# Moving all transposes of a chunk-selected attention and gated MLP kernel from the matmul engine to the DMA crossbar

## The chip, the cores and the metric

The kernel runs on one core of one Trainium2 chip. The metric is the device time of one execution, in microseconds (us), as the median of several executions. Some executions fall into a slower state of the chip; here one counts as slow when it took over 1.5% longer than the fastest of the same kernel.

The names of the engines are those of the profile. PE is the matmul engine, PEld its weight load, DVE the vector engine, ACT the scalar engine, POOL the general engine (GpSimd), SP the sync engine, which here only starts DMAs.

## The reference, cut to what matters

For each of 4 batches there are 8 heads with 768 tokens and 64 columns. An attention picks, for each query, 6 of 24 key chunks by an upper bound on the score. Its output goes through a gated MLP that mixes over tokens.

```python
k_min, k_max = min and max of k over each chunk of 32 keys
ub   = sum_d maximum(q*k_min, q*k_max)            # bound for each query and chunk
sel  = the 6 chunks with the largest ub among the causal ones
mask = sel & (key <= query)
attn = softmax(where(mask, q.k / 8, -1e9)); x = attn @ v      # [768, 512] a batch
h = relu(x @ w_in); u, v = h[:, :512], h[:, 512:]
v_n = (v - mean(v)) / sqrt(var(v) + 1e-6)
v_s = w_spatial @ v_n + b_spatial[:, None]        # mixes tokens
out = (u * v_s) @ w_out
```

## The kernel before

Work goes in pairs of heads, 4 pairs a batch, 16 in all. `prep(i)` makes the operands of pair `i` and its selection, `attend(i)` does scores, exponentials and the product with v. The MLP of a batch is cut into pieces that are put between the attention steps of the next batch; the MLP of the last batch runs alone at the end.

Every transpose is done by PE: it multiplies by an identity, the result lands in PSUM, and DVE or ACT copies it to SBUF.

```python
def load(i):                                  # 6 loads a pair, 96 KB each, issued by POOL
    for hi in range(2):
        nc.gpsimd.dma_start(out=kp[:, :, hi, :], in_=view(k))
        nc.gpsimd.dma_start(out=qs[:, :, hi, c0:c0 + D], in_=view(q))
        nc.gpsimd.dma_start(out=vt[:, :, hi, 0:D], in_=view(v))

def prep(i):
    for t in range(NQT):                      # keys: 6 blocks of 128x128
        nc.tensor.transpose(tr[:, t * P:(t + 1) * P], kp[:, t, :, :], identity)
    ... # DVE: chunk max and min from tr; ACT: keys from tr into kh
    ... # queries: 6 blocks on PE; DVE: relu(q), relu(-q)
    ... # PE: bound ub; DVE: top 6, selection written into free columns of qs
    for hi in range(2):                       # queries + selection: 12 blocks
        for t in range(NQT):
            nc.tensor.transpose(tr[:, t * P:(t + 1) * P], qs[:, t, hi, :], identity)
        nc.vector.tensor_copy(ah, tr)

def attend(i):
    ...
        mm(sc[:, col:col + n], lhsT=kh[hi][:, t * P:(t + 1) * P], rhs=a[hi][:, q0:q0 + n],
           start=True, stop=not dg)
        if dg:                                # causal triangle, added by a matmul
            mm(sc[:, col:col + P], lhsT=identity, rhs=tri, start=False, stop=True)
    nc.scalar.activation(out=e[...], in_=sc[...], func=Act.Exp, scale=scale)
    ... # PE: e @ v; DVE: divide; PE + DVE: 6 blocks of x transposed into xT

# MLP of a batch; the gate comes out already transposed (columns on partitions)
def s_piece(db):
    for (t0, t1) in HALVES:                   # 512 and 256 tokens
        for si in range(NQT):
            mm(vs[:, 0:t1 - t0], lhsT=st["vn"][:, si, db * P:(db + 1) * P], rhs=wsT[:, si, t0:t1], ...)
        mm(vs[:, 0:t1 - t0], lhsT=brow_l, rhs=brow[:, t0:t1], start=False, stop=True)   # bias
        nc.vector.tensor_tensor(st["gT"][:, db, t0:t1], in0=vs[...], in1=st["uT"][...], op=Alu.mult)

load(0); load(1); load_weights(); prep(0)
for i in range(NPAIR):
    load(i + 2); prep(i + 1); attend(i)
    if i == 1: prep_weights()                 # 36 blocks of w_spatial, on PE
    ...                                       # MLP pieces of the batch before
```

The softmax here doesn't subtract the row's maximum and nothing guards it: scores larger than these inputs give would overflow.

## Time and profile before

The median of the three runs is 289.61 us (288.96 to 293.75).

| before | value | view |
|---|---|---|
| span, busy PE / DVE / ACT / POOL | 287.5; 222.4 / 170.7 / 154.3 / 98.1 us | page, part 1 |
| granted clock over the run | 0.976 | clock of the core |
| first exponential; the first one of the pair's second head | 27.5; 44.0 us | timeline of ACT |
| first MLP step of the four batches | 86.9, 147.3, 207.5, 257.1 us | timeline of ACT |
| data moved by DMA | 18.86 MB in 80,590 packets | page, part 2 |

These are the parts of the page of before on which the argument rests. In the line below the span each engine has its busy time, its share of the span and its number of instructions. In the rows below it, each digit is one of 40 slices of the span and gives the busy share in tenths (0 is under a tenth). The DMA row gives the same for the mean of the core's 16 DMA engines, and the last lines give packets, MB and the time of the packets as a share of 16 engines' span.

```profile
span 287.5 us, 5812 instructions
PE 222.4 (77%) x2340; PEld 144.9 (50%) x2340; DVE 170.7 (59%) x498; ACT 154.3 (54%) x217; POOL 98.1 (34%) x150
PE   0037028787879798989798989978888989799994
PEclk9999758999999999999999999999999999999999
DMA  0999997879996667558984848079220000140005
q0 software_dynamic: 77104, 12.20, 57.3%
q1 hardware_dynamic: 3460, 6.30, 6.0%
kp<-in_k_dram POOLq DMA_DIRECT2D x32, 96.0 KB, 3.3
```

From the seventh slice on, PE is busy 70 to 90% in nearly every slice, and at nearly the full clock. The loads of q, k, v and the weights are in queue q0. Their packets occupied 57.3% of the span's DMA time, and the DMA row falls under 9 in most slices from the thirteenth on: DMA had room. A load of 96 KB landed 3.3 us after its issue.

These are lines of the timeline of before in its first 45 us, with start, duration, engine, operation and, in brackets, the idle time ahead and what ended it.

```profile
27.51 1.02 ACT L217 ACTIVATE e<-sc 128x1024 f16<-128x1024 f32 x1 [8.57 <-PE sc L216]
35.13 0.83 POOL L140 DMA_DIRECT2D kp<-in_k_dram  x1 [5.43 <-DMA ws_raw<-in_moe_w_spatial_dram]
40.09 0.20 PE L177 MATMUL acc<-km,rq 128*128 128x48 f16 x1 [11.01 <-POOL km L161]
44.02 1.02 ACT L217 ACTIVATE e<-sc 128x1024 f16<-128x1024 f32 x1 [11.96 <-PE sc L216]
```

The start has a hole: after the first head's exponentials ACT idles until 44.0 us. POOL's later load issues wait until the weight loads have landed, and the small `km` product on POOL stands behind them; PE waits 11.0 us for `km` before it goes on to the second head's scores.

### The profile page before, as it was taken

The page shows a single profiled execution, that of the slowest core. Times are in us where ns is not written, and L with a number is a line of the kernel's source. Part 1 is how long each engine was busy: PE and PEld are TensorE (multiplying, and loading weights), DVE is VectorE, ACT ScalarE, POOL GpSimd, SP SyncE. Part 2 cuts the span into 40 slices and gives each one's busy share as a digit, 9 for nine tenths or more (in the row PEclk, how much of TensorE's full clock was granted, in tenths as well). Part 3 has the DMA queues.
Part 4 walks back from the last instruction along what each step waited for, and adds up shares of the span by engine and source line. Part 5 has one row for each costly group of instructions (what it writes and reads, how often), then busy time and mean ns, then how long its engine had stood idle before and what let it go on. Part 6 is the DMA issues. An engine that isn't in the chain of part 4 may idle for free.

```text
span 287.5 us, 5812 instructions
## 1 busy us (share of the span) xinstructions
PE 222.4 (77%) x2340; PEld 144.9 (50%) x2340; DVE 170.7 (59%) x498; ACT 154.3 (54%) x217; POOL 98.1 (34%) x150
## 2 busy tenths in 40 slices
PE   0037028787879798989798989978888989799994
PEld 0025016666655565655465656655546565544551
DVE  8337005888788875565579865474688654238330
ACT  1021405775785868146878674086878660656213
POOL 9995264546562434124243424051200000000000
PEclk9999758999999999999999999999999999999999
DMA  0999997879996667558984848079220000140005
GB/s 1 65 120 199 194 127 52 56 49 71 70 65 41 46 41 47 37 64 65 204 55 31 55 31 57 0 81 222 16 15 3 0 2 0 39 182 2 0 0 219
DMA packets 80590, 18.86 MB, mean 66 GB/s; under 512 B 75698, under 2 KB 76978, under 8 KB 80564
## 3 DMA queue, kind: packets, MB, share of 16 engines
q0 software_dynamic: 77104, 12.20, 57.3%
q1 hardware_dynamic: 3460, 6.30, 6.0%
q8 instruction: 18, 0.29, 0.4%
q14 instruction: 8, 0.07, 0.1%
HBM read 24.39 MB, written 6.29 MB: 107 GB/s over the span
## 4 chain that ended last, share of the span: by engine, by line
PE 50%; ACT 23%; DMA 8%; POOL 7%; DVE 7%; issue 3%; ACTq 0%; DVEq 0%; POOLq 0%
ACT e L217 13%; PE acc L322 11%; PE sc L213 7%; PE acc L310 7%; DMA w_out_sb<-in_moe_w_out_dram 6%; PE acc L224 5%; PE acc L333 5%; PE acc L285 5%; DVE stats L289 2%; PE tr L234 2%; POOL kp L140 2%; PE sc L216 2%; DMA out_dram<-o 2%; ACT uT L312 2%; PE acc L324 2%
## 5 line engine op out<-in xcount | busy, mean ns | idle before, releaser
L217 ACT ACTIVATE e<-sc 128x1024 f16<-128x1024 f32 (+1 forms) x96 | 84.0, 916 | 44.0 <-PE sc L216 42.9
L140 POOL DMA_DIRECT2D kp<-in_k_dram x32 | 26.7, 839 | 54.1 <-PE tr L152 48.0
L224 PEld LDWEIGHTS <-e 128*128 128x128 f16 x672 | 27.0, 98 | 31.3 <-ACT e L217 17.8
L216 PE MATMUL sc<-tri,identity 128*128 128x128 f16 x192 | 39.5, 222 | 0.0
L336 ACT COPY o<-acc 128x512 f32<-128x512 f32 x24 | 14.0, 585 | 46.9 <-PE acc L333 44.8
L322 PE MATMUL acc<-wsT,vn 128*128 128x512 f16 (+1 forms) x192 | 37.2, 325 | 0.4 <-ACT uT L312 0.2
L325 DVE TENSOR_TENSOR gT<-acc,uT 128x512 f16<-128x512 f32 (+1 forms) x32 | 17.8, 557 | 20.0 <-PE acc L324 18.8
L155 DVE TENSOR_REDUCE kmm<-tr 128x24 f16<-128x768 f16 x16 | 15.3, 953 | 20.4 <-PE tr L152 20.3
L322 PEld LDWEIGHTS <-vn 128*128 128x128 f16 x192 | 18.2, 98 | 12.2 <-issue 1.1
L310 PE MATMUL acc<-xT,w_in_sb 128*128 128x512 f16 (+1 forms) x128 | 23.4, 325 | 0.9 <-ACT uT L312 0.7
L333 PE MATMUL acc<-w_out_sb,gT 128*128 128x512 f16 x96 | 23.1, 378 | 0.4 <-ACT o L336 0.3
L216 PEld LDWEIGHTS <-identity 128*128 128x128 f16 x192 | 19.0, 99 | 7.4 <-issue 5.7
L285 PE MATMUL acc<-w_in_sb,xT 128*128 128x512 f16 x96 | 22.2, 379 | 0.0
L177 PE MATMUL acc<-km,rq 128*128 128x48 f16 x160 | 9.6, 188 | 15.9 <-POOL km L161 14.5
L152 PE MATMUL tr<-identity,kp 128*128 128x128 f16 x96 | 10.0, 229 | 14.7 <-DMA kp<-in_k_dram 14.6
L312 ACT ACTIVATE uT<-acc 128x512 f16<-128x512 f32 (+1 forms) x32 | 14.3, 488 | 12.4 <-PE acc L310 12.3
L289 DVE BATCH_NORM_STATS2 stats<-vraw 128x6 f32<-128x512 f32 x24 | 16.6, 694 | 6.1 <-ACT vraw L287 6.1
L227 DVE RECIPROCAL rec<-acc 128x6 f32<-128x6 f32 x32 | 6.1, 190 | 22.9 <-PE acc L224 22.9
L287 ACT ACTIVATE vraw<-acc 128x512 f32<-128x512 f32 x24 | 14.3, 597 | 9.6 <-PE acc L285 9.6
L180 DVE TENSOR_TENSOR acc<-acc,cmask 128x40 f32<-128x40 f32 x16 | 3.3, 208 | 25.6 <-PE acc L177 22.7
L161 POOL TENSOR_TENSOR km<-kmm,hmask 128x48 f16<-128x48 f16 x32 | 8.3, 276 | 26.3 <-DVE kmm L155 22.6
L310 PEld LDWEIGHTS <-w_in_sb 128*128 128x128 f16 x128 | 12.1, 97 | 9.7 <-issue 1.3
(236 smaller groups left out, 452.0 us busy)
## 6 DMA issues: line engine op xcount, KB each, us to landing
out_dram<-o SPq DMA_DIRECT2D x24, 256.0 KB, 2.0
kp<-in_k_dram POOLq DMA_DIRECT2D x32, 96.0 KB, 3.3
qs_90<-in_q_dram POOLq DMA_DIRECT2D x12, 96.0 KB, 3.3
vt_96<-in_v_dram POOLq DMA_DIRECT2D x12, 96.0 KB, 3.0
ws_raw<-in_moe_w_spatial_dram POOLq DMA_DIRECT2D x1, 1152.0 KB, 15.1
w_in_sb<-in_moe_w_in_dram POOLq DMA_DIRECT2D x1, 1024.0 KB, 10.3
qs_98<-in_q_dram POOLq DMA_DIRECT2D x10, 96.0 KB, 3.2
vt_104<-in_v_dram POOLq DMA_DIRECT2D x10, 96.0 KB, 3.1
```

What stands on the lines that cost most here:

```text
L140: nc.gpsimd.dma_start(out=kp[:, :, hi, :], in_=view(k))
L213: mm(sc[:, col:col + n], lhsT=kh[hi][:, t * P:(t + 1) * P], rhs=a[hi][:, q0:q0 + n], start=True, stop=not dg)
L216: mm(sc[:, col:col + P], lhsT=identity, rhs=tri, start=False, stop=True)
L217: nc.scalar.activation(out=e[:, BASES[g]:BASES[g] + WIDTHS[g]], in_=sc[:, 0:WIDTHS[g]], func=Act.Exp, scale=scale)
L224: mm(avv[:, qi, :], lhsT=e[:, c:c + P], rhs=vt[:, t, hi, 0:D + 1], start=(t == 0), stop=(t == qi))
L285: mm(hv, lhsT=x[:, ko, bi * P:(bi + 1) * P], rhs=w_in_sb[:, ko, DH:DFF], start=(ko == 0), stop=(ko == NDO - 1))
L289: nc.vector.bn_stats(stats, st["vraw"][:, bi, :])
L310: mm(hu[:, 0:t1 - t0], lhsT=w_in_sb[:, ko, db * P:(db + 1) * P], rhs=x[:, ko, t0:t1], start=(ko == 0), stop=(ko == NDO - 1))
L312: nc.scalar.activation(st["uT"][:, db, t0:t1], hu[:, 0:t1 - t0], func=Act.Relu)
L322: mm(vs[:, 0:t1 - t0], lhsT=st["vn"][:, si, db * P:(db + 1) * P], rhs=wsT[:, si, t0:t1], start=(si == 0), stop=False)
L325: nc.vector.tensor_tensor(st["gT"][:, db, t0:t1], in0=vs[:, 0:t1 - t0], in1=st["uT"][:, db, t0:t1], op=Alu.mult)
L333: mm(o_ps, lhsT=st["gT"][:, db, ti * P:(ti + 1) * P], rhs=w_out_sb[:, db, :], start=(db == 0), stop=(db == KO - 1))
```

## The change

The intent was to take from PE everything that is not a product of data, and to remove the hole at the start:

- All transposes go to the DMA crossbar, started by SP: keys, queries, queries with selection, x, w_spatial, and (new) the gate. Keys then come to SBUF, so that DVE and no longer ACT copies them to their places.
- POOL zeroes the triangle in the exponentials, in place of 192 matmuls that add a large negative number to the scores.
- The MLP has tokens on partitions throughout, so its bias is a scalar of a partition. The gate `g` must then be transposed to `gT` before the output matmul, 4 blocks for each 128 tokens.
- There is one load for each tensor and pair (192 KB, 3 a pair); loads and preparation run one pair further ahead; in the program, the weight loads come after the first attention.

The core of the diff, with cuts:

```diff
+    def transpose(out_, in_):
+        nc.sync.dma_start_transpose(out=out_, in_=in_)
...
-        for t in range(NQT):
-            nc.tensor.transpose(tr[:, t * P:(t + 1) * P], kp[:, t, :, :], identity)
+        transpose(kT..., kp...)                       # 6 blocks
+        transpose(qT..., qp...)                       # 6 blocks
-        nc.scalar.copy(kh[0][D:2 * D, :], tr[0:D, :])
-        nc.scalar.copy(kh[1][0:D, :], tr[D:2 * D, :])
+                nc.vector.tensor_copy(dst[:, sp], kT[s0:s1, hi])      # 4 a pair
+            nc.vector.tensor_copy(qs[:, hi, :, d0:d1], qp[:, 2 * j + hi])
...
-        for hi in range(2):                           # selection on PE, copied by DVE
+        a = sb.tile([P, 2, S], F16, tag="a", name="a", bufs=3)
+        transpose(a..., qs...)                        # 12 blocks
...
-                    if dg:
-                        mm(sc[:, col:col + P], lhsT=identity, rhs=tri, start=False, stop=True)
+            for c0, n, w in ((0, 4, 512), (1920, 2, 384)):
+                nc.gpsimd.affine_select(out=blk, in_=blk, compare_op=Alu.is_ge, fill=0.0, ...)
...
+        def s_piece(ti):                              # tokens on partitions
+                nc.vector.scalar_tensor_tensor(g, in0=vs, scalar=bT[:, ti:ti + 1], in1=st["u"][:, ti, :],
+                                               op0=Alu.add, op1=Alu.mult)
+                gT = ml.tile([P, KO, P], F16, tag="gT", name="gT", bufs=3)
+                transpose(gT, g)                      # 4 blocks
...
+        pieces += [s_piece(0), s_piece(1)]
+        for ti in range(2, NQT):
+            pieces += [o_piece(ti - 2), s_piece(ti)]
+        pieces += [o_piece(NQT - 2), o_piece(NQT - 1)]
...
-    load(0); load(1); load_weights(); prep(0)
+    load(0)                                           # ahead of the constants
+    load(1); prep(0); load(2); prep(1)
-    # attend(i) follows load(i + 2) and prep(i + 1)
+    # attend(i) follows load(i + 3) and prep(i + 2); weights are loaded after attend(0)
```

## The prediction

> **What bounds the kernel now.** The matmul engine, in steady state. The table by stretches shows PE busy 16.6 to 18.6 us of every 20 us from 80 to 240 us (DVE 10.5 to 16.4, ACT 10.0 to 16.4). The chain of waits gives PE 50%, ACT 23%. Two other losses. The start: up to 40 us PE is busy 8.2 us; the timeline shows the first exponential at 27.5 us, then a hole to 44.0 us, because POOL's queue waits for the weight loads (w_in, ws_raw, w_out) before later loads and before the small km products. The end: from 252 us the last batch's MLP runs alone, 35 us. A batch in steady state takes about 60 us (first MLP matmul at 148.3, the next at 208.4 us).
>
> **What is removed.** PE: all transposes (k, q, selection, x, w_spatial) and the triangle and bias matmuls. Columns: 13,960 to 8,680 for a pair of heads, 58,400 to 55,300 for an MLP. At the trace's pace (512 columns every 0.21 us) about 200 us of issue fall to about 158. ACT: 32 key copies, 25.5 us; 154 to about 130. DVE: copies of transposes out of PSUM, 30 us; the rq operations become cheaper from SBUF. POOL: 96 load issues of 0.84 us become 48 of perhaps 0.9 to 1.6.
>
> **What is added.** DVE: key, km and query copies, about 1.6 us a pair, so DVE stays near 170 us, and becomes the busiest engine. POOL: 64 triangle operations; from the 128x768 select's 0.8 us I estimate 0.4 to 0.7 us each, 35 us, between exponential and PV matmul. SP: 94 crossbar transposes, 612 blocks of 128x128, 20 MB, and each link from load to scores now has two DMA latencies (loads land in about 3.3 us). The look-ahead of two pairs should cover these.
>
> **Cost of the crossbar.** No trace shows it. The Trainium skill, "DMA: Bandwidth & Descriptors", Latency and other measured facts, has 261 GB/s: 77 us for 20 MB, harmless. "VectorE: DVE Perf Modes", The three transpose paths, has 1309 ns for one block; if that were the rate and not a latency, 612 blocks would take 800 us. I take something near the former. Loads: the start moved 11 of 96 KB in 10 us, so all 96 need at most 87 us of DMA; the sum with transposes and stores stays under 200 us.
>
> **On the critical path.** Start: weights are issued after the first attention, so no hole: first exponential near 21 us, saving about 18 us. First batch's attention alone 32 us. Three batches with MLP: PE 39, DVE 41 us of work, with dependences 46 to 50 each. Tail: 31 us (23 of matmul, with gT latency and the last store). Sum about 226; I add 10 for queueing on SP, whose order is fixed.
>
> **Predicted: 236 us, range 206 to 300. Faster by over 2%: 0.77; within 2%: 0.07; slower: 0.16.**
>
> **What would show it.** PE busy 150 to 175 us; ACT 125 to 135; DVE 160 to 185 and leading; POOL 80 to 120; period of a batch 46 to 52 us; no exponential gap over 5 us before 45 us; transposes landing in 2.5 to 5 us. Wrong, if PE waits mostly for transposed tiles (a, kT, gT, xT), or the SP queue is occupied nearly all the time.
>
> **What would make it wrong.** A transpose occupying SP or the DMA engines over about 0.4 us a block: then 612 blocks alone take 245 us and the gain is gone. One late tile blocking others on SP. POOL operations slowed by DVE copies on a shared SBUF port, delaying the PV matmuls. Faster than the range: DVE overlaps completely, periods near 42 us.

## More of the kernel before

The rounds of the experiments ran on different chips of this kind, each with the kernel before beside them.

"Granted clock" is the share of PE's full clock that the profile shows as granted.

## The result, and the profile after

The changed kernel is correct, and slower: 307.55 us (median of 4 runs, 306.61 to 309.39), against 289.64 us for the kernel before (4 runs, 288.96 to 293.75; the longest of these counts as slow). The ratio is 1.063, with a 95% interval of 1.057 to 1.070. A ratio in this text is the mean time of one kernel's fast runs over that of the other's fast runs of the same rounds, so it is not quite the ratio of the medians.

The same parts of the page, for the kernel after:

```profile
span 306.1 us, 4449 instructions
PE 195.2 (64%) x1552; PEld 100.2 (33%) x1552; DVE 179.8 (59%) x598; ACT 126.2 (41%) x177; POOL 88.3 (29%) x125
PE   0000671713556697784778985879599887797682
PEclk9999977595757599998597997899789999999798
DMA  9999799999999999989999949394910425310243
q0 software_dynamic: 76336, 12.19, 62.3%
q1 hardware_dynamic: 85584, 26.36, 47.4%
kp<-in_k_dram POOLq DMA_DIRECT2D x16, 192.0 KB, 6.4
```

The work left PE, as was meant: 2,340 matmuls became 1,552, and PE's busy time fell from 222.4 to 195.2 us although its granted clock was lower (0.867 over the run, against 0.976). ACT fell by 28 us, POOL by 10, and DVE rose by 9. The direction of these changes is the predicted one. Yet PE's row now begins to fill only at the fifth slice and has holes at the seventh, ninth and tenth. The DMA row is at 9 in nearly all of the first 24 slices. The loads moved the same bytes in nearly the same number of packets (76,336 against 77,104), but the time of these packets grew from 57.3% of 287.5 us (165 us) to 62.3% of 306.1 us (191 us). The hardware queue, which had only the stores (17 us), now takes 145 us.

Where the time lies in the span is seen from four moments: the first exponential, the first MLP step of each batch (the start of its first relu on ACT), and the end. They were read from the timelines of ACT.

| us | first exponential | to first MLP step | from batch to batch | last MLP | span |
|---|---|---|---|---|---|
| predicted | 21 | 32 | 3 times 46 to 50 | 31 | 226 + 10 |
| before | 27.5 | 59.4 | 60.5, 60.2, 49.6 | 30.4 | 287.5 |
| after | 33.2 | 72.4 | 62.1, 58.0, 43.1 | 37.3 | 306.1 |

So after loses 19 us before its first MLP step and 7 us in the last MLP, gains 6.5 us in the third interval, and hardly moves the first two.

The next lines are the busy times of before in two stretches: the stretch, its length, then busy us of PE, PEld, DVE, ACT and POOL with the number of instructions, the granted clock, the DMA share (over 1 where packets of several queues were under way at once), and GB/s.

```profile
40.00:100.00 60.00, 48.50 (x685) 35.96 (x685) 45.41 (x149) 40.75 (x51) 30.97 (x46) 0.95 0.91 60
0.00:207.00 207.00, 152.05 (x1769) 104.00 (x1770) 129.39 (x392) 113.61 (x151) 96.24 (x145) 0.97 0.84 75
```

The same stretches of after:

```profile
40.00:100.00 60.00, 29.83 (x307) 18.41 (x308) 32.71 (x121) 20.81 (x24) 26.65 (x35) 0.67 1.63 160
0.00:207.00 207.00, 117.69 (x1010) 63.23 (x1011) 142.50 (x502) 79.88 (x107) 78.16 (x106) 0.84 1.46 147
```

From 40 to 100 us no compute engine of after was busy more than 55% of the time, and DMA moved 160 GB/s at a share of 1.63. That stage is not bound by a compute engine's work. The waits of after say for what PE waited: engine and tile, what it waited for, total us, times, longest one. ("issue" is time for which the profile shows no wait.)

```profile
PEld L297 <- DMA gT<-g: 25.7, 14, 3.6
PE mlp L297 <- DMA gT<-g: 20.1, 12, 3.1
PE sc L203 <- DMA a<-qs_81: 18.0, 2, 16.0
POOL kp L106 <- DMA kT<-kp: 18.1, 6, 8.8
PE sc L203 <- DMA a<-qs_84: 11.2, 1, 11.2
```

Two different things stand here. The wait for `gT` is many short waits of about 2 us: PE gets to the output matmul before the gate is transposed. The waits for `a` are few and long: scores wait 11 or 16 us for a transpose of the selection. The line of POOL shows the same lateness going back to the loads: the buffer for the next keys comes free only when the crossbar has read the keys.

The DMA issues of after show how long each kind took from issue to landing: number of issues, then KB where there is a size, then the median in us.

```profile
gT<-g SPq DMA_TRANSPOSE x24, 2.4
kT<-kp SPq DMA_TRANSPOSE x16, 5.5
wsT<-ws_raw SPq DMA_TRANSPOSE x6, 7.8
a<-qs_83 SPq DMA_TRANSPOSE x4, 8.4
xT<-x_727 SPq DMA_TRANSPOSE x1, 6.8
xT<-x_2903 SPq DMA_TRANSPOSE x1, 2.8
```

The two lines of `xT` are the same work, 6 blocks: 6.8 us for the last pair of the first batch and 2.8 us for the last pair of all, when there are no more loads. So lateness goes with the loads (or with the other transposes, which end then too; e2 and e9 below separate the two). The timeline of SP in after says the same of the issue itself:

```profile
20.75 6.73 SPq L84 DMA_TRANSPOSE a<-qs_81  x1
182.54 1.43 SPq L84 DMA_TRANSPOSE a<-qs_84  x1
255.19 1.19 SPq L84 DMA_TRANSPOSE gT<-g  x1
```

Issuing a transpose of 12 blocks kept SP for 1.43 us at 182 us, and for 6.73 us at 20.75 us, when the first bursts of loads were under way. SP's later issues wait behind it: it is one queue in a fixed order.

### The profile page after: what moved, and what is told of

Same layout as the page of the kernel before. It is cut to its first block, busy times and chain, and to the rows that moved or that the text cites. A ratio compares the mean times of both kernels' runs of the same rounds, so it can differ in the third digit from the quotient of the medians.

```text
span 306.1 us, 4449 instructions
## 1 busy us (share of the span) xinstructions
PE 195.2 (64%) x1552; PEld 100.2 (33%) x1552; DVE 179.8 (59%) x598; ACT 126.2 (41%) x177; POOL 88.3 (29%) x125
## 3 DMA queue, kind: packets, MB, share of 16 engines
q0 software_dynamic: 76336, 12.19, 62.3%
## 4 chain that ended last, share of the span: by engine, by line
PE 34%; DVE 25%; DMA 24%; SPq 6%; ACT 5%; issue 3%; POOL 2%; POOLq 0%; ACTq 0%; DVEq 0%
DMA gT<-g 11%; PE mlp L260 11%; PE mlp L282 8%; SPq L84 6%; PE acc L218 5%; PE mlp L297 5%; DMA a<-qs_84 5%; PE sc L203 5%; ACT e L205 4%; DMA xT<-x_727 2%; DVE vn L274 2%; DVE kmm L150 2%; DVE kmm L151 2%; DMA xT<-x_443 2%; DVE g L285 2%
## 5 line engine op out<-in xcount | busy, mean ns | idle before, releaser
L205 ACT ACTIVATE e<-sc 128x1024 f16<-128x1024 f32 (+1 forms) x96 | 83.4, 918 | 105.5 <-PE sc L203 103.9
L211 POOL TENSOR_SCALAR_AFFINE_SELECT e<-e 128x512 f16<-128x512 f16 x64 | 33.4, 541 | 114.2 <-ACT e L205 114.1
L260 PE MATMUL mlp<-w_in_sb,xT 128*128 128x512 f16 x192 | 49.0, 399 | 4.5 <-DMA xT<-x_443 3.1
L282 PE MATMUL mlp<-vn,wsT 128*128 128x512 f16 x144 | 40.2, 416 | 5.4 <-DVE vn L274 4.9
L297 PE MATMUL mlp<-w_out_sb,gT 128*128 128x512 f16 x96 | 27.7, 411 | 20.4 <-DMA gT<-g 20.1
L285 DVE SCALAR_TENSOR_TENSOR g<-mlp,bT,u 128x512 f16<-128x512 f32 x24 | 17.6, 747 | 29.2 <-PE mlp L282 29.2
L260 PEld LDWEIGHTS <-xT 128*128 128x128 f16 x192 | 18.3, 101 | 26.1 <-DMA xT<-x_443 3.3
L150 DVE TENSOR_REDUCE kmm<-kT 128x24 f16<-128x768 f16 x16 | 15.1, 943 | 14.4 <-DMA kT<-kp 14.4
L282 PEld LDWEIGHTS <-wsT 128*128 128x128 f16 x144 | 14.8, 105 | 25.2 <-issue 13.5
L106 POOL DMA_DIRECT2D qp<-in_q_dram x16 | 16.5, 1032 | 21.2 <-DVE rq L165 17.4
L203 PE MATMUL sc<-a,kh_0_89 128*128 128x512 f16 (+3 forms) x32 | 8.5, 391 | 18.7 <-DMA a<-qs_81 18.0
L203 PE MATMUL sc<-a,kh_0_95 128*128 128x512 f16 (+3 forms) x32 | 7.5, 348 | 12.2 <-DMA a<-qs_84 11.2
```

The costliest lines, as they stand in the source:

```text
L106: nc.gpsimd.dma_start(out=dst[:, 0:n], in_=src[b, 2 * hp:2 * hp + n].rearrange("h (so si) d -> si h so d", si=P))
L150: nc.vector.tensor_reduce(kmm[:, 0, :], kTc, axis=AX.X, op=Alu.max)
L205: nc.scalar.activation(out=e[:, BASES[gs]:BASES[gs] + WIDTHS[gs]], in_=sc[:, 0:WIDTHS[gs]], func=Act.Exp, scale=scale)
L211: nc.gpsimd.affine_select(out=blk, in_=blk, compare_op=Alu.is_ge, fill=0.0, base=0, channel_multiplier=-1, pattern=[[0, n], [1, P]])
L260: mm(h, lhsT=x[:, ko, ti * P:(ti + 1) * P], rhs=w_in_sb[:, ko, half * DH:(half + 1) * DH], start=(ko == 0), stop=(ko == NDO - 1))
L282: mm(vs, lhsT=wsT[:, si, ti * P:(ti + 1) * P], rhs=st["vn"][:, si, :], start=(si == 0), stop=(si == NQT - 1))
```

## The experiments

The theories after reading the traces were these. First: the crossbar as such is too slow or too late for these chains. Second, as its rivals: (a) the gate's chain in the new MLP costs the time; (b) loads and transposes share the DMA engines and delay each other; (c) the mask on POOL costs it; (d) the lower granted clock costs it. In the texts, LATENCY stands for the first theory in its form of round trips and SP's fixed order, GATE for (a), DMA for (b), MASK for (c), and LAYOUT for the new layout and order of the preparation. The experiments tried (a) to (c); (d) was not tested. All were correct, except for the two that say that they are wrong. Each was executed four times; the numbers given are medians of all four with lowest and highest, then the ratio of the fast ones to the kernel before in the same rounds, with its 95% interval. One execution of e7, e9, e12, e13 and e16 was slow; without it their medians are 303.85, 260.26, 287.89, 291.86 and 287.87 us. Against before, the differences of e10, e11, e15, e16 and e17 are not clear of 2%.

### Is it the crossbar as such? e1 and e6

In e1 every transpose of after goes back to PE; the rest of after stays (mask on POOL, tokens on partitions, loads). DVE copies `a`, `xT` and `wsT` out of PSUM, ACT copies the keys and `gT`; PE's transposes need two of PSUM's small buffers, so that attention and MLP share two in place of having two each, as in before.

```diff
-        transpose(kT..., kp...)
+        kT = pe_transpose(kp...)          # read from PSUM; queries likewise
-        transpose(a..., qs...)
+            nc.vector.tensor_copy(a[:, hi, :], pe_transpose(qs[:, hi]...))
-                transpose(gT, g)
+                nc.scalar.copy(gT..., pe_transpose(g))
```

> The changed kernel with every transpose back on the matmul engine (and copies out of PSUM); loads, triangle mask, gate and order as changed. Theory DMA (load packets and transposes together fill the 16 DMA engines until about 200 us) and theory LATENCY (round trip of a transpose and the in-order SP queue set the pace, full engines or not) both expect 250 to 275 us, below the kernel before, as the start-up and POOL-mask gains remain. Theory MASK (the POOL operation between exponential and PV matmul is the loss) expects over 295.

Measured: 310.32 us (307.81 to 312.01), 1.067 (1.060 to 1.074); the kernel before had 291.03 us. With no crossbar at all the kernel is not faster than after (1.063). So giving the transposes back to PE does not bring the lost time back, and theories DMA and LATENCY both missed their 250 to 275 us. (The number is as theory MASK had it, but e3, below, refutes that cause.) Either the crossbar is not what costs it, or PE's transposes cost as much in this structure. The stages say the second: e1 reaches its first MLP step at 90.9 us, 15 us earlier than after (105.6), and then loses that again in intervals of 68.9 and 68.4 us (62.1 and 58.0 in after). The loads are those of after, and without transposes beside them they land sooner (6.4 us in after):

```profile
kp<-in_k_dram POOLq DMA_DIRECT2D x16, 192.0 KB, 4.1
```

Their packets took 53.6% of 306.1 us, 164 us, where they took 191 us in after.

e6 does the same and also takes the MLP of before, so that no gate needs to be transposed.

> Every transpose on PE (as in the first of these runs) and the MLP of before as well: left of the change are the triangle mask on POOL, the loads, and the preparation's layout and order. Theory GATE expects 268 to 290 us. Theory LAYOUT expects 300 or more.

Measured: 299.65 us (298.61 to 301.45), 1.034 (1.028 to 1.039), above the range of theory GATE. Compared with e5, below, which is the same kernel with the crossbar (287.53 us), the crossbar is 12 us better. With this MLP the crossbar as a whole is a gain. The first theory, that the crossbar as such loses the time, falls for the run as a whole. It loses time mainly at the start: the first MLP step is at 96.0 us in e6 and at 105.5 us in e5.

### The gate's chain: e5, e7 and e13

e5 is after with the MLP of before: the gate comes out transposed from the matmul, the bias is a matmul again, and 24 transposes of 4 blocks go away.

```diff
-        def s_piece(ti):        # tokens on partitions, then transpose(gT, g)
+        def s_piece(db):        # columns on partitions, as before
```

> The changed kernel with the MLP of the kernel before (features on partitions, bias as a matmul, no transpose of the gate); all other parts as changed, crossbar transposes included. The first four runs showed that the crossbar traffic is one loss (31 us when the loads are gone) but not the only one, as taking all transposes back to PE did not help. Theory GATE (the new MLP adds the chain spatial matmul, DVE, transpose, output matmul, and PE waits in it) expects 283 to 297 us. Theory LAYOUT (the new preparation: key, km and query copies by head and block, and its order) expects 303 to 312, as nothing of that is changed here.

Measured: 287.53 us (285.97 to 287.89), 0.989 (0.984 to 0.995). This part of the change alone accounts for 20 us (307.55 to 287.53; the two are of different rounds, and their ratios to before are 1.063 and 0.989). The last MLP went from 37.3 to 30.1 us, and the first two intervals from 62.1 and 58.0 to 55.7 and 49.8 us. The time to the first MLP step did not change (105.5 us in e5, 105.6 in after), so that is another matter.

e7 goes the other way: before with the changed MLP, and the gate transposed by PE and copied by ACT.

> The kernel before with the changed MLP alone, its gate transposed on PE and copied by ACT. Theory GATE expects 298 to 312 us against 290. Theory LAYOUT expects 284 to 294.

Measured: 304.42 us (302.89 to 308.49), 1.048 (1.041 to 1.054). Tokens on partitions cost 14 us in a kernel without any crossbar transpose. So this layout is costly without the crossbar too. Whether the added link costs it there, or the work that PE and ACT get with it, e7 does not separate.

e13 keeps all of the changed MLP and its crossbar transposes, and changes only the order: all six spatial pieces come before all six output pieces, with six `gT` buffers in place of three.

```diff
-        pieces += [s_piece(0), s_piece(1)]
-        for ti in range(2, NQT):
-            pieces += [o_piece(ti - 2), s_piece(ti)]
-        pieces += [o_piece(NQT - 2), o_piece(NQT - 1)]
+        pieces += [s_piece(ti) for ti in range(NQT)] + [o_piece(ti) for ti in range(NQT)]
```

> The changed kernel with all six spatial pieces of a batch ahead of all six output pieces (four to six pieces between the gate's transpose and its use instead of two), six gT buffers instead of three. If the MLP's loss is PE waiting for gT: 287 to 297 us, gT waits under 8 us in the list of waits. If it is the form of the MLP otherwise: 302 to 312.

Measured: 292.03 us (290.52 to 295.35), 1.003 (0.995 to 1.010). The waits of e13 have these lines for the gate:

```profile
PEld L297 <- issue: 13.1, 11, 6.5
DVE g L285 <- DMA gT<-g: 11.8, 8, 5.1
PE mlp L297 <- DVE g L285: 9.4, 4, 6.2
```

PE's direct waits for the transposed gate (20.1 us in after) no longer appear among the waits listed, and the last MLP is 32.3 us instead of 37.3. A part only moved: DVE now waits for the crossbar before it overwrites `g`, and PE for DVE. The distance of two pieces was too short for a link of 0.75 us on DVE plus 2.4 us of crossbar; the order, with the buffers that it needs, is worth about 15 us, most of the 20 us that the layout cost. This isolates the cause better than e5 does: work, bytes and number of transposes are unchanged.

### Loads and transposes on the same DMA engines: e2, e9, e4 and e10

e2 is after with loads for the first four pairs only; later pairs use the same tiles again. Its result is wrong (relative error 1.02). The work of all engines, and of the crossbar, stays.

```diff
+        if g >= NB:
+            loaded[g] = loaded[g - NB]
+            return
```

> The changed kernel, with loads of q, k, v for the first four pairs only; later pairs reuse them (wrong result on purpose). All 94 transposes stay. Theory DMA expects 245 to 270 us, transposes landing in under 3.5 us after 60 us, and an MLP period under 52 us. Theory LATENCY expects 290 or more. Theory MASK expects 295 or more, less a few us as POOL issues no loads.

Measured: 276.67 us (275.15 to 278.79), 0.953 (0.947 to 0.959). The loads cost the changed kernel 31 us, though they are prefetched by three pairs. Theory LATENCY, with its 290 or more, misses; theory DMA has the direction, but its range ends at 270 us, and the first interval is 57.3 us, not under 52. The first MLP step comes at 89.6 us, about where e1 has it (90.9): before it, taking away the later loads and taking away all transposes give back the same 15 to 16 us. The loss there needs both.

e9 does the same to e5, so that the gate's chain is gone also. Its result too is wrong.

> The changed kernel with the old MLP (287.5 us) and loads of q, k, v for the first four pairs only (wrong result on purpose). If the two losses, gate chain and shared DMA engines, add up: 250 to 262 us, as removing the loads took 31 us from the changed kernel. If they overlap: 265 us or more. In either case transposes of kT and xT land in under 3.5 us once the first loads are in.

Measured: 260.63 us (258.87 to 263.97), 0.900 (0.894 to 0.905). That is 27 us less than e5. The lines of its page and DMA issues to set beside those of after:

```profile
DMA  9999959998966743664797195706843110430006
kT<-kp SPq DMA_TRANSPOSE x16, 2.8
a<-qs SPq DMA_TRANSPOSE x16, 4.0
xT<-x SPq DMA_TRANSPOSE x16, 2.7
wsT<-ws_raw SPq DMA_TRANSPOSE x6, 2.8
```

With most of the loads gone the same transposes land in 2.7 to 4.0 us (medians), where medians and single issues were 3.6 to 9.4 us in the loaded part of after. The intervals between batches are 47.2, 48.2 and 43.3 us, and the last MLP takes 30.0 us: this is what the prediction had for the steady state (46 to 50, and 31). So with the two causes taken away the predicted pace is there. What stays apart from the prediction is the beginning: 33.7 us to the first exponential and 54.7 us from there to the first MLP step, where the first loads and the weights are still there.

The shortcoming of e2 and e9 is that they also take away 36 load issues from POOL. POOL was busy 51.2 us in e9 against 88.0 in e5. That POOL's time matters here was not tested alone, but two runs speak against it as the main part: e3 takes 33 us from POOL (55.7 us busy) and is slower than after (though PE gets 192 matmuls there), and e1 gains its 15 us before the first MLP step with POOL as busy as in after (89.1 us).

e4 adds crossbar work without adding a link: each selection transpose is issued twice, the second time into a spare tile that nobody reads.

```diff
+        spare = sb.tile([P, 2, S], F16, tag="spare", name="spare")
+        transpose(spare..., qs...)
```

> The changed kernel with each transpose of the selection tile issued twice, the second to a spare tile nobody reads: 192 more blocks of 128x128, 6.3 MB. Theory DMA expects 25 to 45 us more (6.3 MB at the 160 GB/s that the trace shows while the engines are full is 39 us). Theory LATENCY expects under 10 us more, as nobody waits for the spare and SP is idle nearly half of the time. Theory MASK expects under 5.

Measured: 328.43 us (325.98 to 329.26), 1.129 (1.122 to 1.135). 192 blocks more cost 21 us over after, 0.11 us a block or 1.3 us an issue, between what DMA and LATENCY expected. This is far below the 0.4 us that the prediction named as fatal, but it is time on the critical path, whereas the prediction took the transfers as hidden. The 16 issues also held SP, for at least 1.5 us each in the trace of e4, so this run does not tell the DMA engines' time from SP's.

e10 asks whether the loads only come at the wrong moment. It is e5 with the loads of pairs 2 and 3 held back until selection tiles 0 and 1 have landed, and the weights until tile 2 has; a copy of one element on POOL makes the wait.

```diff
+            if g in gate:
+                nc.gpsimd.tensor_copy(dst[:, 0, 0, 0:1], gate[g][:, 0, 0:1])
             nc.gpsimd.dma_start(out=dst[:, 0:n], in_=...)
```

> The changed kernel with the old MLP, where the loads of pairs 2 and 3 wait until the selection tile of pair 0 and 1 has landed, and the weights until that of pair 2 has. All traffic stays, only the start is unloaded. If the first transposes are late because they share DMA engines with a dozen loads: first exponential at 20 to 26 us instead of 34.9, total 275 to 283 us. If the crossbar is slow by itself: first exponential after 30 us, total 285 to 292.

Measured: 295.02 us (293.22 to 295.44), 1.020 (1.014 to 1.025), so 7.5 us worse than e5. The first exponential came at 25.0 us instead of 34.9, as hoped, but the first MLP step at 112.6 instead of 105.5. The timeline of SP in e10:

```profile
18.76 1.27 SPq L84 DMA_TRANSPOSE a<-qs  x1
30.18 1.45 SPq L84 DMA_TRANSPOSE a<-qs  x1
38.40 1.41 SPq L84 DMA_TRANSPOSE a<-qs  x1
```

The first selection now issues in 1.27 us and lands 3.6 us after its issue began (12.0 us in e5). The third, at 38.4 us, meets the loads that were held back: it issues fast but takes 10.3 us to land. Pacing moved the collision, it did not remove it; the weights, moreover, were now late (`wsT` is first transposed at 66.5 us, at 52.1 us in e5).

### The mask on POOL: e3, e8 (and e18 below)

e3 is after with the triangle added by PE again.

```diff
+                    if dg:
+                        mm(sc[:, col:col + P], lhsT=identity, rhs=tri, start=False, stop=True)
-                nc.gpsimd.affine_select(out=blk, in_=blk, compare_op=Alu.is_ge, fill=0.0, ...)
```

> The changed kernel with the triangle mask back as matmuls on PE, no POOL operation on the exponentials. Theories DMA and LATENCY expect 300 to 318 us (PE gets 192 matmuls, but has slack). Theory MASK expects 290 or less.

Measured: 316.54 us (316.05 to 317.58), 1.089 (1.083 to 1.094). In after, the mask on POOL is worth 9 us.

e8 does it to before: mask on POOL, nothing else.

> The kernel before with the triangle mask on POOL alone (192 matmuls less on PE, 64 selects on the exponentials more). In the changed kernel the mask on POOL was worth 9 us. Here PE is the busiest engine in steady state, so 275 to 286 us are expected; 290 or more if the way exponential, POOL, PV matmul is worth more than the matmuls.

Measured: 304.43 us (303.64 to 306.27), 1.050 (1.045 to 1.056). There it costs 14 us. From the page and the waits of e8:

```profile
PE 220.3 (73%) x2148; PEld 136.8 (45%) x2148; DVE 171.2 (57%) x498; ACT 153.5 (51%) x217; POOL 130.3 (43%) x214
PEld L227 <- POOL e L220: 20.7, 27, 1.8
```

This is above the expected 275 to 286 us. 192 matmuls left PE and its busy time hardly fell (222.4 to 220.3), while PE's weight loads now waited for POOL, which also issues 96 loads in this kernel (130.3 us busy, from 98.1). In before the same weight loads waited for ACT instead, and not much less:

```profile
PEld L224 <- ACT e L217: 17.8, 30, 1.6
```

So these waits do not account for the 14 us by themselves. The sign of this part depends on the rest: it is a gain in after (48 load issues on POOL) and in e14, and a loss in before (96). Why it turns is not shown.

This also accounts for e1 and e6, as an estimate and no more. If costs add, e6 should be before (290) plus the mask (14) less the early start (5, see e11), so 299; 299.65 was measured. e1 adds the gate (14) and should be 313; 310.32 was measured.

### The early start: e11

e11 is before with its loads ahead of the constants, and the weights loaded after the first attention, as in after.

> The kernel before with the change's start only: first loads issued ahead of the constants, weights after the first attention. Nothing else changes. The trace of before has a hole from 31.4 to 44.0 us and starts its first exponential at 27.5; expected first exponential at 18 to 22 us, no hole over 5 us, total 272 to 280 us. If the hole only moves: 284 to 290.

Measured: 283.6 us (282.99 to 284.14), 0.981 (0.977 to 0.985). The hole is gone, as predicted, but it was worth 5 us, not 18: the first exponential came at 26.3 us, not at 18 to 22, the first MLP step at 80.2 us instead of 86.9, and the interval from first exponential to first MLP step only fell from 59.4 to 53.9 us. From 28 to 44 us PE was busy 3.5 us in before and 8.8 us in e11: PE has work for only half of that stretch even without the hole, and these 5 us are about what was gained.

### Which transposes should go to the crossbar? e12, e14, e17, e15, e16 and e18

These start from e5 (287.53 us, MLP of before) or from e11 and change which transposes the crossbar does.

e12 puts the selection, 192 blocks, on PE, and DVE copies it from PSUM. (The text gives a wrong number of blocks that remain: it is 324 of 516.)

> The changed kernel with the old MLP and the selection tile transposed on PE with DVE copies; keys, queries, outputs and w_spatial still by the crossbar (420 blocks instead of 516). PE waited directly 35 us for this tile with the old MLP. If those waits are what is left: 272 to 282 us. If they only move to kT, qT and xT, or DVE (18 us more) becomes the limit: 285 or more.

Measured: 288.85 us (285.96 to 290.4), 0.996 (0.989 to 1.003), so no gain over e5. Its page:

```profile
PE 206.1 (72%) x1856; PEld 121.8 (43%) x1856; DVE 201.6 (70%) x645; ACT 126.7 (44%) x185; POOL 89.0 (31%) x127
DVE  5799999009999899999996999746268424218330
```

DVE rose to 201.6 us and is at 9 or near it in nearly all slices from the tenth to the twenty-fifth. This fits DVE losing what the DMA engines got back; it was not tested alone.

e14 puts keys and queries on PE, the same number of blocks. They are read from PSUM directly, and ACT copies the keys, as in before. The selection, x and w_spatial stay with the crossbar.

```diff
-        transpose(kT..., kp...)
+        kT = pe_transpose(kp...)
-                nc.vector.tensor_copy(dst[:, sp], kT[s0:s1, hi])
+                nc.scalar.copy(dst[:, sp], kT[s0:s1, hi])
```

> The changed kernel with the old MLP, keys and queries transposed on PE and read from PSUM, key copies on ACT; selection, outputs and w_spatial by the crossbar (324 blocks instead of 516, as few as the run with the selection on PE less 96). DVE gets no new work. If DMA traffic is the limit until 200 us: 268 to 281 us. If PE or the order is: 285 to 300, as with all transposes on PE (299.7).

Measured: 278.64 us (277.1 to 280.38), 0.957 (0.949 to 0.964). This is the fastest correct kernel. The count of blocks in the text has the same flaw as that of e12. Its page:

```profile
PE 201.9 (73%) x1856; PEld 122.5 (44%) x1856; DVE 166.5 (60%) x549; ACT 157.0 (56%) x249; POOL 88.6 (32%) x127
DMA  9999959999999959491999995717842210160005
q1 hardware_dynamic: 46148, 16.92, 33.4%
```

The two kernels have the same crossbar traffic (16.92 MB in the hardware queue) and the same PE work. They differ in who pays for the rest: DVE 201.6 us and ACT 126.7 in e12, DVE 166.5 and ACT 157.0 in e14. They also differ in which link of the chain stays on the crossbar, and in the number of transposes that SP issues (54 and 38). So fewer crossbar blocks alone are not the gain (e12); which of the three differences makes it in e14 was not separated.

e17 moves x also to PE, with its copy on DVE.

> As the best kernel so far, with the attention outputs transposed on PE too; only the selection and w_spatial stay on the crossbar (228 blocks instead of 324; DVE 9 us more, PE 96 transposes more). If DMA traffic is still the limit: 270 to 276 us. If PE and DVE now matter as much: 277 to 284.

Measured: 298.01 us (296.31 to 299.53), 1.025 (1.018 to 1.032), 19 us worse than e14, for 96 blocks, and above both expectations. So "less crossbar" is not the rule either. DVE went from 166.5 to 180.0 us; that this is the whole reason was not tested.

e15 adds the crossbar for x and w_spatial to e11.

> The kernel before with the early start (283.6 us), and only attention outputs and w_spatial by the crossbar: 132 blocks, each needed late. PE loses 132 transposes, DVE 12 us of copies. Expected 274 to 282 us; 284 or more if even this traffic delays the loads or the first MLP matmuls.

Measured: 285.95 us (284.51 to 288.64), 0.985 (0.976 to 0.993). e11 had 0.981. In that structure the move is worth nothing that can be seen. Why it is worth 19 us in e14 against e17 and nothing here stays open.

e16 paces the loads of e14, with selection tile 0 for pairs 2 and 3, and tile 1 for the weights.

> The best kernel so far (old MLP, keys and queries on PE: 278.6 us), with the loads of pairs 2 and 3 held until the selection tile of pair 0 has landed and the weights until that of pair 1 has. If the engines are no longer full after the start: first exponential at 21 to 26 us instead of 37.7, total 266 to 275 us. If they still are, as with the full traffic: 278 us or more.

Measured: 287.99 us (285.07 to 290.05), 0.985 (0.975 to 0.996), 9 us worse than e14. The first two selections of e16 land 3.8 and 3.7 us after their issues began. The timeline of SP shows the third:

```profile
40.28 5.62 SPq L91 DMA_TRANSPOSE a<-qs  x1
```

It takes 5.62 us to issue and 16.9 us to land, and PE's scores wait 15.4 us for it. This is as in e10: a burst that is held back collides with the next transposes.

e18 is e14 with the triangle on PE.

> The best kernel so far (278.6 us) with the triangle mask back as matmuls on PE. If the mask on POOL is a gain because PE is relieved of 192 matmuls: 283 to 290 us. If it is a loss because exponential, POOL and PV matmul form a chain in which PE waits: 266 to 275 us.

Measured: 290.4 us (289.08 to 292.73), 1.007 (0.9995 to 1.014). In e14 the mask on POOL is worth 12 us, though e8 had it as a loss in before.

## Why the prediction was wrong

| us | first exponential | to first MLP step | from batch to batch | last MLP | span |
|---|---|---|---|---|---|
| predicted | 21 | 32 | 3 times 46 to 50 | 31 | 226 + 10 |
| after | 33.2 | 72.4 | 62.1, 58.0, 43.1 | 37.3 | 306.1 |
| e1, all on PE | 23.2 | 67.7 | 68.9, 68.4, 44.9 | 33.1 | 306.1 |
| e13, gate used later | 33.2 | 70.5 | 61.3, 51.5, 41.4 | 32.3 | 290.2 |
| e5, old MLP | 34.9 | 70.6 | 55.7, 49.8, 45.2 | 30.1 | 286.2 |
| e2, few loads (wrong result) | 33.3 | 56.3 | 57.3, 49.6, 43.2 | 37.4 | 277.1 |
| e9, old MLP, few loads (wrong result) | 33.7 | 54.7 | 47.2, 48.2, 43.3 | 30.0 | 257.1 |
| e11, before started early | 26.3 | 53.9 | 60.5, 60.5, 49.6 | 30.4 | 281.3 |
| e14, best | 37.7 | 52.0 | 62.3, 52.5, 43.7 | 30.1 | 278.3 |

**What was right.** The work moved as predicted. ACT fell to 126.2 us (125 to 135 predicted), DVE was 179.8 (160 to 185), POOL 88.3 (80 to 120), while PE, and not DVE, stayed the busiest with 195.2 us against 150 to 175, part of it at a lower clock. Of the signs of failure that the prediction named, the first came true: 63 of the 106 us of waits that the profile lists for PE's matmuls are for transposed tiles (`a` 38, `gT` 20, `xT` 5). The second came true at the start only: SP was occupied for about 157 us by issues of transposes (the sum of their durations; 111 us in e9), half of the span, but for 72 of the 88 us from 20 to 108 us.

**The step that failed: "the sum with transposes and stores stays under 200 us", and so "harmless".** The prediction costed the transposes at 77 us (an estimate from the skill page's 261 GB/s) and the loads at no more than 87 us, compared the sum with the whole span, and concluded that DMA is hidden. Three things were wrong in it.

First, the size of the terms. By the page's measure (time of the packets, over 16 engines) the loads (weights included) already took 165 us in before, which the prediction had on the page and did not use; it inferred 87 us from one burst at the start. In after they took 191 us, and the hardware queue 145 us, of which the stores are about 17 (from before), so the transposes about 128. The sum is 336 us, where under 200 was predicted. Packets that are under way together count each, so this is not a lower bound on time, but the DMA row at 9 in nearly all of the first 24 slices says that the engines had little room.

Second, the comparison with the whole span. Loads and most transposes fall into the first 207 us, at a DMA share of 1.46. Third, the kind of cost. A transpose is not a background transfer but a link of the chain load, keys, selection, scores, x, MLP. What it loses to loads beside it (`kT` 5.5 us instead of 2.8, an issue of 6.73 us instead of 1.43) goes into the chain several times a pair. e2 and e9 show that the loads (with their issues on POOL) cost 31 and 27 us with everything else in place, e1 and e2 that before the first MLP step the loss needs loads and transposes together, and e4 that crossbar work that is added costs time although nobody waits for its result.

The Trainium skill, "DMA: Bandwidth & Descriptors", section "Issuing engines are not separate DMA queues", says that DMAs started by different engines run on the same 16 DMA engines and interleave. The prediction cited another section of that page; it did add loads and transposes up as work of the same engines, but did not reckon that each delays the other. The runs agree with it: loads come from POOL and transposes from SP, and yet each slows the other (`kp` lands in 6.4 us in after and 4.1 in e1, `kT` in 5.5 us in after and 2.8 in e9). The same section calls the time on the issuing sequencer usually small relative to the DMA. Here it was 1.19 us of 2.4 for `gT`, and with loads beside it up to 6.73 us for one issue, so for transposes the measurement decides against it.

**The term that was missing: the gate.** The prediction had "dependences 46 to 50 each" for a batch, and "31 us (23 of matmul, with gT latency and the last store)" for the tail. The tail measured 37.3 us and the first two intervals 62.1 and 58.0. e13 shows why: the gate's link (0.75 us on DVE, 2.4 us of crossbar) was used after two pieces, and the output matmuls that waited for it (20.1 us) stood ahead of PE's other work. More distance alone gave back 15 us, with the same transposes on the crossbar. The layout is dearer on PE as well: e7 lost 14 us with it.

**The start.** "No hole: first exponential near 21 us, saving about 18 us" was wrong twice. In after the first selection took until about 32 us, because its transpose was issued at 20.75 us into the burst of loads (SP held for 6.73 us; PE waited 16.0 us). That burst held a weight load as well: POOL's timeline has `w_in` (1,024 KB) at 17.4 us, right after the first twelve loads, although the program has it after the first attention; only the other two weights, from 39.7 us on, came after the first exponential. With these loads held back (e10) the first exponential came at 25.0 us. And even where the start went well (e11) the saving was 5 us. "First batch's attention alone 32 us" was never seen: the runs of this table show 52 to 72 us, and the three kernels of them with all transposes on PE, before, e11 and e1, 59.4, 53.9 and 67.7. That term was too small by 20 us or more in every case, crossbar or not. It and the late start are most of what stays between e9 (260.6 us) and the prediction (236): 13 us and 23 us, of which a faster third interval and the 10 us for queueing give some back.

**The crossbar's cost per block.** The prediction left open whether the 1309 ns in the Trainium skill, "VectorE: DVE Perf Modes", section "The three transpose paths", would be a rate, and took it not to be. That was right: 12 blocks land in 4.0 us in e9, and e4's 192 blocks more cost 0.11 us each. The prediction's condition for failure ("over about 0.4 us a block") was not met in the mean (157 us on SP for 612 blocks, 0.26 us each), only beside the loads (6.73 us for 12 blocks, 0.56 us each), and it failed all the same: what had to be watched was not the mean but what happens beside the loads. Another of its conditions, one late tile blocking others on SP, is what the trace shows at 20.75 us.

**The clock.** From 40 to 100 us the granted clock was 0.67 in after and 0.95 in before. The Trainium skill, "TensorE: Matmul & The Clock Gate", section "Why this matters for your kernels", advises against PE idle gaps of over about 3 us because throughput then drops. The trace agrees in direction: in that stretch PE was busy 29.8 of 60 us. That the lower clock follows from the holes and adds to them is a reading, not shown; how much of the 19 us before the first MLP step it accounts for was not separated by any run.

**What stays open:** the share of the clock; why the mask on POOL costs 14 us in before and gains 9 to 12 us in after and e14; why x on the crossbar is worth 19 us in one structure (e14 against e17) and nothing in another (e11 against e15); how much of the gain of e2 and e9 is POOL's time; how much of e4's 21 us is SP's and how much the DMA engines'; which difference makes e14 10 us faster than e12; and what holds the first stage of e9 at 88 us.

## What to carry to other kernels

Cost a move to DMA like a move to a busy engine: read from the page how long packets of the loads already take, in the stage where the new transfers will fall, and take each transfer that is a link of a chain with its landing time under load, not with bytes over bandwidth. Give a new link more distance between its producer and its consumer before anything else, for the reordering of e13 cost only three more buffers and gave 15 us. When a change has many parts, try them apart: of this one the best kernel (e14, 278.64 us, 4.3% under before) keeps the crossbar for the selection, x and w_spatial, the mask on POOL and the early loads, and gives up the new MLP layout and the crossbar for keys and queries.

## What the Trainium skill lacked or had wrong

- "DMA: Bandwidth & Descriptors", "Issuing engines are not separate DMA queues": it calls the sequencer's time to start a DMA usually small relative to the DMA. The issue of a crossbar transpose from SP took 1.19 us for 4 blocks (of 2.4 us to landing) and 1.43 us for 12, and beside a burst of loads 6.73 us for 12 (after).
- "DMA: Bandwidth & Descriptors", "Latency and other measured facts": its 261 GB/s for transposes comes without a figure for transposes beside loads. With the loads of this kernel the same 6 blocks landed in 5.5 us instead of 2.8 (`kT`, after and e9), and all DMA together moved 147 GB/s over the first 207 us.
- "VectorE: DVE Perf Modes", "The three transpose paths": the 1309 ns for a 128x128 block are not said to be a latency. With several blocks in one issue, 6 landed in 2.7 us and 12 in 4.0 us (medians of e9), and 192 more blocks cost 0.11 us each in the whole kernel (e4).
- No page was found with the time of a triangle select on POOL: it took 541 ns in the mean over the two sizes used here (64 of them, 33.4 us in after).
